# Agent attention and a squared-ReLU MLP on one core: key pieces three blocks apart, value pieces about nine, the cast of the exponentials on VectorE

## The chip, the core and the metric

The kernel runs on one core of one Trainium2 chip. The metric is the device time of one execution, in microseconds (us). The engines are named as the profile names them: PE is TensorE's matmuls, PEld its weight loads, DVE is VectorE, ACT is ScalarE, POOL is GpSimd, SP is SyncE, which here issues the DMAs.

## What is computed

The reference, cut to what matters (B = 4 batches, 12480 rows in each, 128 columns, 49 agents, 49920 tokens, a hidden width of 2048):

```python
def sm(a, b):
    s = scale * (a @ b.transpose(0, 2, 1))
    s = s - s.max(-1, keepdims=True)
    e = np.exp(s)
    return e / (e.sum(-1, keepdims=True) + 1e-09)
agent_v = sm(agents, k) @ v
x = (sm(q, agents) @ agent_v).reshape(B * S, D)
r = np.maximum(x @ w_in, 0.0)
return (r * r) @ w_out
```

A batch thus has two attention parts. The first goes over all its keys and values and ends in 49 rows, `agent_v`. The second takes its queries to the agents. The MLP then runs over all tokens, and it is nearly all of the matmul work.

## The kernel before

**Tiling.** A supertile is 960 tokens (120 partitions x 8 columns of tokens, `ST`); a batch has 13 of them, the whole run 52. Keys and values come in pieces of the same size, 13 a batch. The hidden width is cut in 16 slices of 128. One slice of one supertile is a block; there are 52 x 16 = 832 blocks, and they are the clock by which everything is ordered.

**A block.** `mm1` (L467) makes 128 x 960 hidden values in PSUM from the query probabilities `p_a`, `p_b` (49 rows) and the weights `w_a`, `w_b`, into which `agent_v @ w_in` has been folded. Products are kept near float32 by splitting each operand in a high and a low part of the type float32r and adding three products. So `mm1` is 6 matmuls of 480 columns and `mm2` 12. ACT does the ReLU (L471) and the square (L475), DVE casts the square to its high part `gh` (L479) and subtracts to get the low part `gl` (L483). `mm2` (L495) follows `LAG` = 6 blocks behind `mm1` and adds up 16 blocks in two PSUM banks, which `store_a` (ACT, L506) and `store_d` (DVE, L510) empty after each supertile.

**Beside the blocks.** For each supertile there is the query work: `q_half` (PE, L195, two halves of the scores), `q_shift` (DVE, L386 and L392), `q_exp` (ACT, L401), `q_total` (DVE, L405 to L409), `q_norm` (POOL, L412), `q_hi` (ACT, L420 and L421), `q_lo` (POOL, L425 and L426), `q_transpose` (PE, L436), `q_copy` (ACT, L442 and L443, into `p_a`) and `q_spread` (two DMAs that copy `p_a` into `p_b`). For batches 1 to 3 the key and value work of the batch is laid among the blocks of the batch before it. Batch 0 has none to hide behind; it is computed ahead of the first block.

**Keys.** Two pieces share one pass (`k_pair`, PE, L195, two halves of 32 small matmuls in the trace); `kp_copy` (ACT, L212) takes the scores to SBUF into `sk`, `kp_max` (DVE, L217) reduces them. After all 13 pieces `k_max` finds the maximum over the batch (L230 to L242).

**Values.** Only then can a value piece be done: `k_sub` (POOL, L245) subtracts the maximum, `k_exp` (ACT, L248) takes the exponential, `k_hi` (ACT, L252) casts it to its high part in the tile `pe`, `k_lo` (POOL, L255) makes the low part; `v_hi` (ACT, L262) and `v_lo` (DVE, L266), two halves each, split the values; `v_acc` (PE, L274, 16 matmuls) and `v_sum` (DVE, L281) add the product up. `a_final` and four `w_make` (L356 to L360) close the batch and make the next `w_a` and `w_b`.

**Order.** A planner writes the order. `at(t, f)` puts a step at block time `t`; `chain` (L534) looks for free places: at most one extra step on ACT, on DVE or on PE in a block (`taken`), and no two users of the attention PSUM banks at once (`banks`; there is one such pair of banks, the tile `ps_att`). All steps are then sorted by time and issued in this order, so each engine's queue has exactly that order. `plan_turns` (L588) places `q_transpose` at least `SLACK` = 5 blocks behind `q_lo`. `plan_batch` (L593) spreads a batch's key pieces and then its value pieces evenly, both by `d = (span - 50) / (2 * NS)`, which is 6.08 blocks for `span` = 208. With that, batch 1's keys end near block 74 of its 208, and its value pieces lie from block 79 to 169.

**Start.** Ahead of block 0, PE computes batch 0's attention, two `w_make`, and the scores of the first three key pieces of batch 1 (`AHEAD` = 3, by `k_scores`, L184, with ACT's L223 and DVE's L226). The weights come as float64 bits and are turned into float32 on DVE by `win_make` and `wo_make` (L91 to L97, seven instructions for each quarter).

Of the kernel before, what the change touches and what calls it, by code (L numbers as in the profile page):

```python
# [25 lines left out]
def agent_attention_relu2_kernel(ctx: ExitStack, tc: tile.TileContext, qT, kT, v, agT, w_in, w_out, outT):  # L26
# [6 lines left out]
    nc = tc.nc  # L33
    C, B, NCH, _ = kT.shape
# [138 lines left out]
    def piece(n):  # L173
        return sk[:, n * G:(n + 1) * G, :]
# [74 lines left out]

    def k_hi(n):  # L250
        pes[n] = wk.tile([CH, G, A2], F32R, name="pe", bufs=3)
        nc.scalar.copy(pes[n][:, :, :A], piece(n))  # L252

    def k_lo(n, eng=nc.gpsimd):
        eng.tensor_tensor(out=pes[n][:, :, A:], in0=piece(n), in1=pes[n][:, :, :A].bitcast(F32), op=ALU.subtract)  # L255
# [261 lines left out]

    LAG = 6
    SLACK = 5
    AHEAD = 3  # L520
    steps = []

    def at(t, f, *args):
        steps.append((t, len(steps), f, args))
# [9 lines left out]
    def chain(t, todo):  # L534

        first = prev = None
        while todo:
            n = 1  # L540
            while todo[0][0] == "PE" and n < len(todo) and (todo[n][1] in reads_bank and todo[n][0] != "PE" or todo[n][1:-1] == todo[n - 1][1:-1]):
                n += 1
            t += hop[prev][todo[0][0]] if prev else 0
            while True:
                g, p, ts = t, None, []
                for e, *_ in todo[:n]:
                    g += hop[p][e] if p else 0
                    while (e, g) in taken:
                        g += 1
                    ts.append(g)  # L550
                    p = e
                held = range(ts[0], ts[-1] + 2) if todo[0][0] == "PE" else ()
                if not any(y in banks for y in held):
                    break
                t += 1
            banks.update(held)
            for (e, f, *args), g in zip(todo, ts):
                taken.add((e, g))
                at(g + .5, f, *args)
            first = ts[0] if first is None else first  # L560
            prev, t, todo = p, ts[-1], todo[n:]
        return first, t
# [23 lines left out]
    ends = {}  # L586

    def plan_turns(s):  # L588
        _, end = chain(max(ends[s] + (1 if s < 3 else SLACK), (s - 1) * NF), [("PE", q_transpose, s), ("ACT", q_copy, s)])
        at(end + .9, q_spread, s)  # L590
        assert end + 3 < s * NF, (s, end)

    def plan_batch(b, base, span):  # L593

        d = (span - 50) / (2 * NS)
        n = AHEAD if b == 1 else 0
        while n < NS:
            m = min(2, NS - n)
            f = k_pair if m == 2 else k_one
            first, end = chain(base + int(n * d), [("PE", f, b, n, 0), ("PE", f, b, n, 1), ("ACT", kp_copy, n, m), ("DVE", kp_max, n, m)])  # L600
            for x in range(m):
                at(max(base, first - 8 + x), k_load, b, n + x)
            n += m
        _, t0 = chain(end + 1, [("DVE", k_max, 0, NS), ("PE", k_max, 2), ("DVE", k_max, 3), ("PE", k_max, 4), ("DVE", k_max, 5)])
        used = {}
        for n in range(NS):
            t = t0 + 1 + int(n * d)
            t2 = max(t + 3, used.get(n - 2, 0))
            first, _ = chain(t2, [("ACT", v_hi, n, 0), ("DVE", v_lo, n, 0)])
            _, t2 = chain(t2 + 1, [("ACT", v_hi, n, 1), ("DVE", v_lo, n, 1)])  # L610
            at(first - 6, v_load, b, n)
            chain(t - (3 if n else 0), [("POOL", k_sub, n)])
            _, t1 = chain(max(t + (2 if n else 3), used.get(n - 3, 0)), [("ACT", k_exp, n), ("ACT", k_hi, n), ("POOL", k_lo, n)])
            used[n], end = chain(max(t1 + SLACK, t2 + 2), [("PE", v_acc, n), ("DVE", v_sum, n)])
        _, end = chain(end + 1, [("DVE", v_join), ("DVE", a_final, 0), ("PE", a_final, 1), ("DVE", a_final, 2), ("DVE", a_final, 3)])
        for f in range(F // 512):
            _, end = chain(end + 2, [("PE", w_make, b, f, 0), ("ACT", w_make, b, f, 1), ("DVE", w_make, b, f, 2)])
        assert end + 2 < base + span, (b, end, base + span)
# [75 lines left out]
    for f in range(2):  # L694
        for x in range(3):
            at(t + 4 + .1 * x + .5 * f, w_make, 0, f, x)
    for n in range(AHEAD):
        at(t + 5 + .1 * n, k_scores, 1, n)
        at(t + 5.5 + .1 * n, k_copy, n)
        at(t + 5.5 + .1 * n, k_pmax, n)  # L700
    for x in range(7):
        at(t + 8 + .1 * x, wo_make, 1, x)
        at(1.52 + x, wo_make, 2, x)
    for x in range(2):
        at(.13 + .01 * x, wo_split, 0, x)
        at(1.56 + .01 * x, wo_split, 1, x)
        at(8.52 + x, wo_split, 2, x)
    at(t + 12, begin)
    at(1.95, warm_up, 3)
    at(3.95, warm_up, 2)  # L710
    plan_queries_early(1, 0, True)
    plan_turns(1)
    for f in range(2, F // 512):
        chain(4 * f - 7, [("PE", w_make, 0, f, 0), ("ACT", w_make, 0, f, 1), ("DVE", w_make, 0, f, 2)])
    _, end = chain(8, [("DVE", wo_make, 3, x) for x in range(7)] + [("ACT", wo_split, 3, 0)])
    at(end + .6, wo_split, 3, 1)
    assert end < 3 * PW // P + LAG
# [49 lines left out]
```

## Time and profile before

| | us |
|---|---|
| median of 3 runs | 2041.16 (2036.58 to 2042.4) |
| the profiled execution | 2041.42 |
| its span in the trace | 2039.6 |
| first ReLU of block 0 (L471) | at 78.15 |
| mean granted PE clock | 0.982 of full speed |

The profiled execution is the one that the rows below are from. 1.8 us of its time lie outside the span. A row of the timeline gives the start, the duration, the engine, the line and the operation, and in brackets how long the engine stood idle ahead of it and what ended that. A row of the stretches ("A:B length, ...") gives each engine's busy time in the stretch with the number of instructions in parentheses, then the granted PE clock, the share of DMA and the GB/s.

### The profile page before, as it was taken

Reading aid. Unit: us, or ns where it says so; the run is one execution under the profiler, and the core shown is the slowest. Engines: PE = TensorE matmul, PEld = TensorE weight load, DVE = VectorE, ACT = ScalarE, POOL = GpSimd, SP = SyncE. Lnnn points to the kernel's source line nnn. Section 1 sums busy time; section 2 is a strip of 40 time slices with the busy share of each in tenths; the row PEclk is TensorE's granted clock in tenths of the full one; section 3 lists DMA queues with packets and bytes.
Section 4 is the critical chain, followed back from the end, with each engine's and each line's share of the span. In section 5 each row is a group of like instructions: output and inputs, shape, how many; then the busy total and the mean of one; then the engine's idle time right before and its main releaser. Section 6 shows DMA issues by size and latency. Waiting matters only on the chain.

```text
span 2039.6 us, 47851 instructions
## 1 busy us (share of the span) xinstructions
PE 1995.0 (98%) x19791; PEld 1871.2 (92%) x19795; DVE 1787.5 (88%) x2267; ACT 1762.3 (86%) x2202; POOL 409.2 (20%) x261
## 2 busy tenths in 40 slices
PE   9899999999999999899999999989999999999998
PEld 8689998889899999898999999989898999999997
DVE  6798899889888889899988888989998898999887
ACT  2488899889888889898988888988998999999997
POOL 2110024443000002444201001245400101010100
PEclk8899999999999999999999999999999999999999
DMA  8321211120021211131011121122110010101000
GB/s 288 110 86 54 76 54 54 57 73 25 28 102 44 77 54 53 57 92 34 24 67 63 47 93 34 56 71 75 34 38 33 28 44 28 44 28 44 28 24 21
DMA packets 38503, 119.40 MB, mean 59 GB/s; under 512 B 4164, under 2 KB 11692, under 8 KB 38284
## 3 DMA queue, kind: packets, MB, share of 16 engines
q1 hardware_dynamic: 38284, 116.33, 17.7%
q8 instruction: 155, 2.54, 0.5%
q14 instruction: 64, 0.52, 0.1%
HBM read 80.97 MB, written 25.56 MB: 52 GB/s over the span
## 4 chain that ended last, share of the span: by engine, by line
PE 88%; ACT 4%; DVE 3%; issue 2%; POOL 2%; POOLq 0%; ACTq 0%; DVEq 0%
PE out L495 50%; PE h L467 24%; PE ps_att L195 7%; POOL pp L426 2%; PE ps_att L436 2%; PE ps_att L274 2%; ACT r L471 2%; ACT g L475 2%; PE h L184 1%; PE out L295 1%; DVE gl L483 1%; PE ps_att L356 1%; PE ps_one L184 1%; POOL e L412 1%; DVE gh L479 1%
## 5 line engine op out<-in xcount | busy, mean ns | idle before, releaser
L483 DVE TENSOR_TENSOR gl<-g,gh 128x960 fp32r<-128x960 f32 x832 | 987.2, 1187 | 0.0
L471 ACT ACTIVATE r<-h 128x960 f32<-128x960 f32 x832 | 810.3, 974 | 177.0 <-PE h L467 147.6
L495 PE MATMUL out<-gh,wo_hi 64*128 64x480 f32 x3328 | 862.6, 391 | 14.3 <-ACT ob L506 12.5
L495 PE MATMUL out<-gl,wo_hi 64*128 64x480 f32 x3328 | 843.4, 379 | 3.2 <-DVE gl L483 3.2
L495 PE MATMUL out<-gh,wo_lo 64*128 64x480 f32 x3328 | 844.4, 380 | 0.0
L475 ACT ACTIVATE g<-r 128x960 f32<-128x960 f32 x832 | 833.1, 1001 | 6.6 <-DVE gl L483 6.2
L479 DVE CAST gh<-g 128x960 fp32r<-128x960 f32 x832 | 596.3, 717 | 195.2 <-ACT g L475 125.6
L495 PEld LDWEIGHTS out<-gh,wo_hi 64*128 64x128 f32 x3328 | 480.6, 186 | 45.7 <-ACT ob L506 18.8
L495 PEld LDWEIGHTS out<-gl,wo_hi 64*128 64x128 f32 x3328 | 482.0, 186 | 21.1 <-DVE gl L483 4.7
L495 PEld LDWEIGHTS out<-gh,wo_lo 64*128 64x128 f32 x3328 | 485.6, 188 | 12.6
L467 PE MATMUL h<-p_a,w_a 49*128 49x480 f32 x1664 | 432.3, 390 | 0.1
L467 PE MATMUL h<-p_b,w_a 49*128 49x480 f32 x1664 | 423.9, 379 | 0.0
L467 PE MATMUL h<-p_a,w_b 49*128 49x480 f32 x1664 | 423.7, 379 | 0.0
L412 POOL TENSOR_TENSOR e<-e,sm 120x392 f32<-120x392 f32 x52 | 67.7, 1302 | 972.8 <-PE out L495 594.1
L467 PEld LDWEIGHTS h<-p_a,w_b 49*128 49x128 f32 x1664 | 242.5, 186 | 17.1
L467 PEld LDWEIGHTS h<-p_a,w_a 49*128 49x128 f32 x1664 | 240.7, 186 | 13.9 <-ACT r L471 4.5
L467 PEld LDWEIGHTS h<-p_b,w_a 49*128 49x128 f32 x1664 | 244.6, 189 | 7.2
L425 POOL TENSOR_TENSOR pp<-e,pp 120x196 fp32r<-120x196 f32 x52 | 89.2, 1715 | 242.2 <-PE out L495 144.4
L195 PEld LDWEIGHTS ps_att<-ag_sb,qt 64*120 64x120 f32 x1632 | 118.8, 186 | 3.0 <-DVE pm L226 0.8
L195 PE MATMUL ps_att<-ag_sb,qt 64*120 64x49 f32 x1632 | 111.7, 262 | 0.4 <-DVE pm L226 0.4
L255 POOL TENSOR_TENSOR pe<-sk,pe 120x392 fp32r<-120x392 f32 x39 | 78.9, 2027 | 151.1 <-PE out L495 112.9
L426 POOL TENSOR_TENSOR pp<-e,pp 120x196 fp32r<-120x196 f32 x52 | 104.0, 2001 | 0.0
(133 smaller groups left out, 1202.4 us busy)
## 6 DMA issues: line engine op xcount, KB each, us to landing
kt<-kT SPq DMA_DIRECT2D x52, 480.0 KB
vt<-v SPq DMA_DIRECT2D x52, 480.0 KB
qt<-qT SPq DMA_DIRECT2D x52, 480.0 KB
outT<-ob SPq DMA_DIRECT2D x51, 480.0 KB
p_b<-p_a SPq DMA_DIRECT2D x104, 91.9 KB
raw<-w_in SPq DMA_DIRECT2D x4, 512.0 KB
raw<-w_out SPq DMA_DIRECT2D x4, 512.0 KB
outT<-ob SPq DMA_DIRECT2D x2, 240.0 KB
```

Source lines behind the costliest of these rows:

```text
L184: nc.tensor.matmul(ps[:CH, c * A:(c + 1) * A], kt[:, c, :], ag_sb[:, b, :], start=True, stop=True)
L195: mm = nc.tensor.matmul(ps[:CH, u, r * A:(r + 1) * A], cols[u][r][rows], ag_sb[rows, b, :], start=x == 0 and r == 0, stop=x == 1 and r == ...
L255: eng.tensor_tensor(out=pes[n][:, :, A:], in0=piece(n), in1=pes[n][:, :, :A].bitcast(F32), op=ALU.subtract)
L412: eng.tensor_tensor(out=es[s], in0=es[s], in1=sms.pop(s).to_broadcast([CH, G, A]), op=ALU.mult)
L425: eng.tensor_tensor(out=pp[:, :H, 64:], in0=e[:, :H], in1=pp[:, :H, :A].bitcast(F32), op=ALU.subtract)
L426: eng.tensor_tensor(out=pp[:, H:, :A], in0=e[:, H:], in1=pp[:, H:, 64:].bitcast(F32), op=ALU.subtract)
L467: nc.tensor.matmul(hs[i][:, t, :TT], w, p, start=n == 0, stop=n == 2)
L471: nc.scalar.activation(rs_[i], hs.pop(i)[:, :, :TT], AF.Relu)
L475: nc.scalar.activation(gs[i], rs_.pop(i), AF.Square)
L479: nc.vector.tensor_copy(ghs[i], gs[i])
L483: nc.vector.tensor_tensor(out=gls[i], in0=gs.pop(i), in1=ghs[i].bitcast(F32), op=ALU.subtract)
L495: mm = nc.tensor.matmul(o[u][:, :TT], w[rows, j, :], g[rows, u, :], start=j == 0 and x == 0 and n == 0, stop=j == NF - 1 and x == 1 and n ...
```

## The change

Four edits, all but one of them in the planner.

```diff
     def k_hi(n):
         pes[n] = wk.tile([CH, G, A2], F32R, name="pe", bufs=3)
-        nc.scalar.copy(pes[n][:, :, :A], piece(n))
+        nc.vector.tensor_copy(pes[n][:, :, :A], piece(n))
...
+    KD, TAIL, EARLY = 3, 46, 4
...
-        _, end = chain(max(ends[s] + (1 if s < 3 else SLACK), (s - 1) * NF), [("PE", q_transpose, s), ("ACT", q_copy, s)])
+        _, end = chain(max(ends[s] + (1 if s < 3 else SLACK + 3), (s - 1) * NF), [("PE", q_transpose, s), ("ACT", q_copy, s)])
...
-        d = (span - 50) / (2 * NS)
-        n = AHEAD if b == 1 else 0
+        n = EARLY if b == 1 else 0
...
-            first, end = chain(base + int(n * d), [("PE", f, b, n, 0), ("PE", f, b, n, 1), ("ACT", kp_copy, n, m), ("DVE", kp_max, n, m)])
+            first, end = chain(base + int(n * KD), [("PE", f, b, n, 0), ("PE", f, b, n, 1), ("ACT", kp_copy, n, m), ("DVE", kp_max, n, m)])
...
+        d = (base + span - TAIL - t0) / (NS - 1)
...
-            _, t1 = chain(max(t + (2 if n else 3), used.get(n - 3, 0)), [("ACT", k_exp, n), ("ACT", k_hi, n), ("POOL", k_lo, n)])
+            _, t1 = chain(max(t + (2 if n else 3), used.get(n - 3, 0)), [("ACT", k_exp, n), ("DVE", k_hi, n), ("POOL", k_lo, n)])
...
-    for n in range(AHEAD):
-        at(t + 5 + .1 * n, k_scores, 1, n)
-        at(t + 5.5 + .1 * n, k_copy, n)
-        at(t + 5.5 + .1 * n, k_pmax, n)
     for x in range(7):
-        at(t + 8 + .1 * x, wo_make, 1, x)
-        at(1.52 + x, wo_make, 2, x)
+        at(t0 + 20.9 + .4 * x, wo_make, 1, x)
+        at(3.6 + .4 * x, wo_make, 2, x)
...
+    at(1.55, k_load, 1, AHEAD)
+    for n, t in ((0, 2.5), (2, 6.5)):
+        for x in range(2):
+            at(t + .6 * x, k_pair, 1, n, x)
+        at(t + 1, kp_copy, n, 2)
+        at(t + 1.05, kp_max, n, 2)
```

First, a batch's key pieces lie 3 blocks apart, a pair thus 6. The value pieces take what is left, `d` about 9.3 to 9.5 blocks apart: those of batch 1 lie from block 49 to 179, where they lay from 79 to 169. Second, `k_hi` goes from ACT to DVE. Third, `q_transpose` keeps three blocks more from `q_lo`; where the banks were taken, the planner went further still. Fourth, the scores of batch 1's first pieces leave the start: four pieces, as two pairs, come in blocks 2 to 7. `wo_make` of the second quarter of `w_out` moves ahead of block 0, that of the third is packed into blocks 3 to 6, the `w_make` of `w_in`'s last two quarters move to blocks 4 and 8, and three of the five filler matmuls in blocks 1 to 3 fall away.

The rows below are each engine's order in the built programs. ACT just ahead of block 0 and in it (a difference, - before, + after; L358 ends `w_make`, L223 copies scores of `k_scores`, L471 is the ReLU, L119 the high part of `w_out`):

```order
 L358 CAST w_a<-ps_one 113x512
 L358 CAST w_a<-h 113x512
-L223 COPY sk<-ps_one 120x392
-L223 COPY sk<-h 120x392
-L223 COPY sk<-ps_one 120x392
 L471 ACTIVATE r<-h 128x960
 L119 CAST wo_hi<-wo_f 128x512
```

The three score copies are gone, and with them three groups of scores on PE; block 0's ReLU follows the `w_make` at once.

ACT among batch 1's value pieces, before (from about block 91; L262 is `v_hi`, L248 the exponential, L252 `k_hi`, L471 and L475 the blocks' own work):

```order
L262 CAST vs_86<-vt 120x4x128
L471 ACTIVATE r<-h 128x960
L475 ACTIVATE g<-r 128x960
L248 ACTIVATE sk<-sk 120x392
L471 ACTIVATE r<-h 128x960
L475 ACTIVATE g<-r 128x960
L252 CAST pe<-sk 120x8x49
L471 ACTIVATE r<-h 128x960
L475 ACTIVATE g<-r 128x960
L248 ACTIVATE sk<-sk 120x392
L471 ACTIVATE r<-h 128x960
L475 ACTIVATE g<-r 128x960
```

and DVE there after (from about block 78; L252 is `k_hi`, L281 `v_sum`, L266 `v_lo`, L479 and L483 the blocks' own):

```order
L483 TENSOR_TENSOR gl<-g,gh 128x960
L479 CAST gh<-g 128x960
L252 CAST pe<-sk 120x8x49
L483 TENSOR_TENSOR gl<-g,gh 128x960
L479 CAST gh<-g 128x960
L281 TENSOR_TENSOR acc<-ps_att,acc 98x516
L483 TENSOR_TENSOR gl<-g,gh 128x960
L479 CAST gh<-g 128x960
L266 TENSOR_TENSOR vs_86<-vt,vs_86 120x4x128
```

`k_hi` is now one of DVE's four extra instructions for a value piece, and ACT's are three where they were four.

ACT around the copy of the transposes of supertile 7, before (L442 and L443 are `q_copy`, which stands right behind `q_transpose` in the plan; L506 is `store_a`):

```order
L442 CAST p_a<-ps_att 113x8x64
L443 CAST p_a<-ps_att 113x8x56
L471 ACTIVATE r<-h 128x960
L475 ACTIVATE g<-r 128x960
L248 ACTIVATE sk<-sk 120x392
L471 ACTIVATE r<-h 128x960
L475 ACTIVATE g<-r 128x960
L252 CAST pe<-sk 120x8x49
L471 ACTIVATE r<-h 128x960
L506 COPY ob<-out_3658 128x480
```

and after (L401 is `q_exp` of supertile 8):

```order
L471 ACTIVATE r<-h 128x960
L506 COPY ob<-out_3747 128x480
L475 ACTIVATE g<-r 128x960
L471 ACTIVATE r<-h 128x960
L475 ACTIVATE g<-r 128x960
L471 ACTIVATE r<-h 128x960
L475 ACTIVATE g<-r 128x960
L401 ACTIVATE e<-e 120x392
L471 ACTIVATE r<-h 128x960
L475 ACTIVATE g<-r 128x960
L442 CAST p_a<-ps_att 113x8x64
L443 CAST p_a<-ps_att 113x8x56
```

The transposes stood three blocks ahead of the store; now they stand three blocks behind it and behind the next supertile's query scores. In the plan that is block 98 before and 104 after, with `q_lo` at block 93 in both, and the first block that uses the result is 112.

More of the change, by code (lines that the diff above doesn't have):

```diff
@@ L706, in agent_attention_relu2_kernel @@
         at(1.56 + .01 * x, wo_split, 1, x)
-        at(8.52 + x, wo_split, 2, x)
+        at(9.52 + x, wo_split, 2, x)
     at(t + 12, begin)
-    at(1.95, warm_up, 3)
-    at(3.95, warm_up, 2)
+    at(1.95, warm_up, 2)
     plan_queries_early(1, 0, True)
     plan_turns(1)
+    at(1.55, k_load, 1, AHEAD)
[4 more added lines that the diff above has]
+        at(t + 1.05, kp_max, n, 2)
     for f in range(2, F // 512):
-        chain(4 * f - 7, [("PE", w_make, 0, f, 0), ("ACT", w_make, 0, f, 1), ("DVE", w_make, 0, f, 2)])
+        for x in range(3):
+            at(4 * f - 3.5 + .1 * x, w_make, 0, f, x)
+    banks.update(range(2, 10))
+    taken.update((e, t) for e in ("ACT", "DVE") for t in (3, 4, 7, 8))
     _, end = chain(8, [("DVE", wo_make, 3, x) for x in range(7)] + [("ACT", wo_split, 3, 0)])
```

## Prediction

> **What bounds the kernel now.** I read the page's shares and the chain that ended last, then the same engines stretch by stretch, then the timeline where a stretch is long.
>
> ```profile
> PE 1995.0 (98%) x19791; PEld 1871.2 (92%) x19795; DVE 1787.5 (88%) x2267; ACT 1762.3 (86%) x2202; POOL 409.2 (20%) x261
> PE 88%; ACT 4%; DVE 3%; issue 2%; POOL 2%; POOLq 0%; ACTq 0%; DVEq 0%
> ```
>
> PE is nearly always busy, but DVE and ACT are not far behind, so a stage can have another limit than the whole. The next rows are stretches of five supertiles among the value pieces of batches 1, 2 and 3, one supertile of batch 2's, one stretch with key pairs, and six supertiles of the last batch, which carry no key or value work. Columns: length, then busy time of PE, PEld, DVE, ACT, POOL.
>
> ```profile
> 275.20:475.40 200.20, 189.95 (x1875) 177.02 (x1872) 184.64 (x228) 180.04 (x242) 88.25 (x40) 0.97 0.20 60
> 776.60:976.70 200.10, 190.43 (x1875) 175.80 (x1873) 184.92 (x229) 180.03 (x242) 89.76 (x40) 0.97 0.20 60
> 1277.90:1478.40 200.50, 190.31 (x1875) 176.88 (x1873) 185.28 (x229) 180.11 (x242) 86.94 (x40) 0.97 0.20 60
> 852.50:896.70 44.20, 39.73 (x377) 37.90 (x375) 36.13 (x47) 36.53 (x51) 23.91 (x8) 0.92 0.17 50
> 624.70:662.20 37.50, 37.50 (x405) 35.91 (x403) 31.52 (x40) 32.75 (x40) 2.79 (x3) 1.00 0.17 59
> 1587.10:1791.30 204.20, 204.20 (x2022) 198.25 (x2020) 185.45 (x229) 191.54 (x229) 20.95 (x18) 1.00 0.11 36
> ```
>
> The ReLU's line alone, cut the same way, counts the blocks (its first row holds 80; the second holds 96 and the start of one more):
>
> ```profile
> 776.60:976.70 200.10, 78.01 (x80) 0.97 0.20 60
> 1587.10:1791.30 204.20, 93.45 (x97) 1.00 0.11 36
> ```
>
> Without key or value work a supertile takes 204.2 / 6 = 34.03 us, and PE has no gap: that is PE's pace. Key pairs keep it so (37.5 of 37.5 us busy). Among value pieces it is different. Five supertiles at PE's pace are 170.2 us; 12 `v_acc` fall in them, and one takes 0.96 us of the chain (row below), 11.5 us together. So PE needs 181.7 us and the stretch takes 200.1: **18.4 us a batch are not PE's work.** A second look at the same rows says why. ACT is busy for 180.0 us and DVE for 184.9, where the work without values takes 191.54 / 6 = 31.9 and 185.45 / 6 = 30.9 a supertile. Three engines need 180 to 185 us each; none can catch up when it has waited. The timeline shows the worst wait:
>
> ```profile
> 845.83 0.96 PE ps_att L274 x16
> ...
> 844.71 5.00 POOL L425 TENSOR_TENSOR pp<-e,pp 120x196 fp32r<-120x196 f32 x1 [2.70 <-ACT r L471]
> 849.68 11.70 POOL L426 TENSOR_TENSOR pp<-e,pp 120x196 fp32r<-120x196 f32 x1
> 861.34 0.94 POOL L245 TENSOR_TENSOR sk<-sk,mM 120x392 f32<-120x392 f32 x1
> ...
> 849.17 0.68 DVE L281 TENSOR_TENSOR acc<-ps_att,acc 98x516 f32<-98x516 f32 x1
> 859.76 1.15 DVE L483 TENSOR_TENSOR gl<-g,gh 128x960 fp32r<-128x960 f32 x1
> 866.96 0.66 DVE L479 CAST gh<-g 128x960 fp32r<-128x960 f32 x1 [6.05 <-ACT g L475]
> ...
> 861.43 0.97 PE L436 MATMUL ps_att<-ident_r,pp 64*113 64x64 f32 x8 [4.47 <-POOL pp L426]
> ```
>
> `q_lo`, two POOL operations, takes 16.7 us; it ends just after DVE has run dry (DVE's last instruction ends at 860.91, POOL's at 861.38). POOL gets on only when DVE leaves it room. PE stood 4.47 us for it, since the transposes are in PE's queue ahead of the blocks; that supertile took 44.2 us.
>
> **The change part by part.**
>
> *Value pieces apart.* They now take 130 blocks (49 to 179), 8.125 supertiles, not 80-odd. PE's own need there: 8.125 x 34.03 + 13 x 0.96 = 289.0 us. What a piece adds on the others comes from the batch 2 row: DVE (184.92 - 5 x 30.9) / 13 = 2.34 us (this holds what POOL takes from it), ACT (180.03 - 5 x 31.92) / 13 = 1.57 us.
>
> *The cast.* ACT is rid of 0.52 us a piece. DVE has no such cast in the trace; the nearest are these:
>
> ```profile
> L252 ACT CAST pe<-sk 120x392 fp32r<-120x392 f32 x39 | 20.3, 521 | 0.0
> L479 DVE CAST gh<-g 128x960 fp32r<-128x960 f32 x832 | 596.3, 717 | 195.2 <-ACT g L475 125.6 <-PE h L467 60.2 <-PE out L495 2.0
> L56 DVE CAST ident_r<-ident 128x128 fp32r<-128x128 f32 x1 | 0.2, 217 | 0.0
> ```
>
> 128 columns take 0.22 us and 960 take 0.72, so 392 take between these, 0.38 on the line through both (217 + 264 x 500 / 832 = 376 ns). Then DVE needs 8.125 x 30.9 + 13 x 2.72 = 286.4 us, 99% of PE's need, where it was 184.9 against 181.7, 102%. ACT: 8.125 x 31.92 + 13 x 1.05 = 273.0 us, 94%, where it was 99%. Queued behind the cast on DVE are the block's own `gh` and `gl`; it waits for the exponential, which ACT does in the same block, as `v_lo` already waits for `v_hi`.
>
> *The transposes.* They stand 11 blocks behind `q_lo` in the plan instead of 5, some 13 us more at 2.2 us a block, against the 4.47 us that PE stood. The 8.2 us that the supertile of 44.2 us took over its need (34.03 + 2 x 0.96 = 35.95) go with it. The cover at the other end: 7 blocks, 15 us, remain until `mm1` needs the result, and the copy into `p_b` must fit; in the start its DMA issue begins at 68.01 and `mm1` reads it at 77.51 without a wait, so it takes at most 9.5 us. If that cover went, PE would stand at the start of each supertile.
>
> *What is left of the 18.4 us.* The other 10.2 us are 2.04 a supertile, from ACT and DVE running at PE's own pace. At 94% and 99% I take half of it, 1.02 x 8.125 = 8.3 us. Bounds: nothing (with DVE at 185.45 of 204.2 us, 91%, PE shows no gap), and 16.6 us if the rate stays. So the value stretch gives back 18.4 - 8.3 = 10.1 us a batch, **30.3 us** in three; bounds 1.8 x 3 = 5.4 and 55.2.
>
> *Key pieces.* Each half costs PE 1.62 us wherever it stands (row below), so bunching them moves no work. At 6 blocks a pair, 2.67 pairs a supertile, PE needs 34.03 + 2.67 x 3.24 = 42.7 us, far above ACT and DVE. Batch 2's first pair stands half a block behind its loads in the plan, but a load waits only for its buffer and for what is ahead in SP's queue, the copy into `p_b` at block 200.9; in the trace loads follow that copy within a microsecond:
>
> ```profile
> 108.03 0.70 SPq L448 DMA_DIRECT2D p_b<-p_a  x1
> 109.34 1.22 SPq L178 DMA_DIRECT2D kt<-kT  x2
> ...
> DMA packets 38503, 119.40 MB, mean 59 GB/s; under 512 B 4164, under 2 KB 11692, under 8 KB 38284
> ...
> kt<-kT SPq DMA_DIRECT2D x52, 480.0 KB
> ```
>
> 480 KB at the 59 GB/s of the whole run are 8.3 us, and 7.6 blocks are 16. Cost: nothing.
>
> *The start.*
>
> ```profile
> 72.12 1.78 PE L184 MATMUL ps_one<-ag_sb,kt 128*120 128x49 f32 x16
> 77.19 0.48 PE L467 MATMUL h<-p_a,w_a 49*128 49x480 f32 x2
> 77.51 0.38 PE L467 MATMUL h<-p_b,w_a 49*128 49x480 f32 x2
> 67.72 0.28 DVE L322 TENSOR_TENSOR acc<-out,acc 49x129 f32<-49x129 f32 x1 [4.58 <-PE out L312]
> 72.08 0.69 DVE L360 TENSOR_TENSOR w_b<-ps_one,w_a 113x512 fp32r<-113x512 f32 x1 [1.82 <-ACT w_a L358]
> 78.36 0.42 DVE L91 TENSOR_SCALAR cv_p<-raw 128x512 uint32<-128x512 uint32 x1
> 83.25 0.65 DVE L479 CAST gh<-g 128x960 fp32r<-128x960 f32 x1
> 68.01 0.85 SPq L447 DMA_DIRECT2D p_b<-p_a  x1
> 78.10:120.70 42.60, 15.62 (x17) 0.84 0.12 41
> 144.44 1.62 PE ps_att L195 x32
> ```
>
> Block 0 began at 77.19, behind three score groups from 72.12 on. Without them it can begin when `w_b` is there, 72.08 + 0.69 = 72.77: 4.4 us earlier. `wo_make` of the second quarter held DVE from 78.36 to 83.25, ahead of block 0's cast; now it lies in the 4.58 us that DVE stood idle ahead of 67.72, so 4.9 us of DVE go from the first blocks. Against that four halves of 1.62 us, 6.5 us, come into them. Blocks 0 to 5 have no `mm2`, and the first 16 blocks took 42.6 us at a clock of 0.84, so PE has room; I take half of the 6.5 as hidden. That is 4.9 - 3.25 = 1.65. And the blocks later carry 9 pieces instead of 10, 1.6 us less. Together **7.6 us**; bounds: nothing hidden, 4.4, or all, 10.9.
>
> **Sum.** 2041.4 (profiled execution, 0.3 us above the median of 2041.16) - 30.3 - 7.6 = 2003.5, **2004 us**. By the bounds: 2041.4 - 55.2 - 10.9 = 1975, and 2041.4 - 5.4 - 4.4 = 2032.
>
> **A rule against it.** The Trainium skill, "SBUF — State Buffer", section "Who interferes with whom", says that GpSimd's only ports are VectorE's second pair, that a VectorE cast in a 2-port mode or an operation with two SBUF inputs holds it for the whole instruction, and that reductions, and operations with at most one SBUF input outside those modes, do not. The trace agrees: L425's 5.00 us ended at 849.71, in `v_sum`, which reads one operand from PSUM, and L426 then sat through casts and subtractions until DVE ran dry. By the rule `k_hi` on DVE shuts POOL out for longer; its outcome is the third rival.
>
> **The rivals.**
>
> 1. *PE alone sets the pace among the values.* For it: DVE at 91% costs nothing today. Against: 99% is not 91%. Then all 55.2 us go: 2041.4 - 55.2 - 7.6 = 1979. Chance 0.18.
> 2. *The waits only move.* POOL's `k_sub` and `k_lo` also wait for room, `k_exp` waits for `k_sub`, and the same 18.4 us a batch come back over more blocks: 2041.4 - 7.6 = 2034. For it: only the transposes get more cover, nothing else. Against: ACT has room now. Chance 0.10.
> 3. *DVE shuts POOL out in every supertile of values.* Then the loss goes with the supertiles, 18.4 / 5 x 8.125 = 29.9 us a batch, 11.5 more than now: 2041.4 + 34.5 - 7.6 = 2068, slower. It decides where DVE's need passes PE's: (289.0 - 286.4) / 13 = 0.2 us more a piece, a cast of 0.58 us instead of 0.38, inside its bounds. Against: between pieces more blocks are bare, and a bare block leaves DVE idle. Chance 0.08.
> 4. *The start brings nothing*, because the pairs hold up the first blocks: 2041.4 - 30.3 = 2011. Chance 0.07, inside the range.
>
> The forecast itself has 0.57.
>
> **How the numbers follow.** A measurement of this kernel can tell about 0.3% from no change, 6 us. Forecast, first and fourth rival are faster, 0.82; the second, 7 us under, lies at the edge: I put 0.05 to faster and 0.05 to no change. Slower has 0.08. The range leaves out half of the first rival at the bottom and the third at the top: 1982 to 2035.
>
> **What would show it.** Right: the value stretches near 297 us for 130 blocks, with PE busy over 97%; no POOL operation of over 10 us for which PE stands; block 0's ReLU near 74; `k_hi` on DVE near 0.38 us in the mean. Wrong: value supertiles over 37.5 us each, long waits for L245 or L255 in place of L426, waits at a supertile's first block, `k_hi` over 0.58 us.

## The result and the profile after

| | before | after |
|---|---|---|
| median of 4 runs, us | 2041.31 (2036.58 to 2042.4) | 2016.66 (2013.45 to 2019.05) |
| ratio, 95% interval | | 0.9883 [0.9859, 0.9906] |
| the profiled execution, us | 2041.42 | 2018.85 |
| its span, us | 2039.6 | 2017.1 |

The change makes the kernel 24.6 us faster, 22.6 by the two profiled executions. The forecast was 37. The page of after, shares and chain:

```profile
PE 1987.2 (99%) x19836; PEld 1869.0 (93%) x19840; DVE 1797.3 (89%) x2306; ACT 1750.2 (87%) x2162; POOL 333.0 (17%) x261
PE 89%; DVE 4%; ACT 3%; issue 2%; POOL 2%; POOLq 0%; ACTq 0%; DVEq 0%
```

The shares hardly tell the two kernels apart: DVE has a percent more of the span and of the chain; ACT has a percent more of the span and a percent less of the chain. POOL's 409.2 us of before, which hold its waiting for DVE inside an instruction, are now 333.0. The stretches tell more. Blocks and stretches are named here after the batch whose key and value work is laid among them: "batches 2 and 3" are blocks 208 to 623. First these 416 blocks of before (from block 208's ReLU to block 624's), then the same blocks of after, its value pieces of batches 2 and 3 (8 supertiles each, 12 `v_acc`), its worst supertile, and six supertiles without key and value work:

```profile
584.10:1587.10 1003.00, 983.13 (x10016) 922.35 (x10014) 885.00 (x1111) 885.07 (x1115) 229.93 (x130) 0.99 0.18 56
```

```profile
575.10:1565.10 990.00, 979.13 (x10016) 925.32 (x10014) 897.35 (x1137) 877.95 (x1088) 186.25 (x130) 0.99 0.18 56
699.40:998.80 299.40, 293.95 (x2895) 277.40 (x2893) 284.04 (x357) 272.24 (x343) 79.70 (x50) 0.98 0.17 52
1196.70:1491.20 294.50, 289.07 (x2893) 274.04 (x2891) 283.19 (x357) 271.99 (x343) 79.80 (x50) 0.99 0.18 53
880.50:922.60 42.10, 41.00 (x383) 37.25 (x381) 37.99 (x46) 34.54 (x44) 10.90 (x10) 0.92 0.13 41
1565.10:1769.10 204.00, 204.00 (x2021) 196.20 (x2019) 183.54 (x229) 191.14 (x229) 17.03 (x18) 1.00 0.11 36
```

PE's own pace is unchanged: 204.0 / 6 = 34.0 us a supertile. For 8 supertiles and 12 `v_acc` of 0.96 us it needs 283.5 us, so the value pieces of batch 2 lose 15.9 us and those of batch 3 lose 11.0, as do those of batch 1 (294.5 us too). Before, batch 2 lost 18.4; the forecast left 8.3.

The waits of before that the change was to remove, PE's wait for `store_a`, and those of after (engine, line, who was waited for: us in total, times, longest):

```profile
PE ps_att L436 <- POOL pp L426: 13.3, 3, 4.5
...
PE out L495 <- ACT ob L506: 12.5, 12, 1.7
...
ACT g L475 <- DVE gl L483: 6.2, 11, 0.9
```

```profile
ACT g L475 <- DVE gl L483: 21.1, 28, 1.4
...
PE out L495 <- ACT ob L506: 12.2, 14, 1.5
...
PE ps_att L195 <- DVE acc L281: 3.0, 3, 1.0
...
ACT pp L420 <- POOL e L412: 0.2, 1, 0.2
```

The transposes' wait is gone, as forecast. `q_hi`, which stands behind POOL's `q_norm`, waits for nothing worth naming. What has grown is another wait: ACT's square waits for a buffer that DVE's `gl` has yet to read, 21.1 us instead of 6.2. DVE is behind. PE itself now stands longest for ACT: `mm2` waits for `store_a` to empty a bank, 12.2 us in all, and 12.5 before. The prediction has no term for this wait, and the change leaves it as it was. The timeline shows where, in the worst supertile. DVE first, then POOL, then PE with its stretches:

```profile
880.17 0.98 DVE L479 CAST gh<-g 128x960 fp32r<-128x960 f32 x1
881.08 0.77 DVE L252 CAST pe<-sk 120x392 fp32r<-120x392 f32 x1
881.77 1.92 DVE L483 TENSOR_TENSOR gl<-g,gh 128x960 fp32r<-128x960 f32 x1
883.62 0.65 DVE L479 CAST gh<-g 128x960 fp32r<-128x960 f32 x1
884.19 1.45 DVE L266 TENSOR_TENSOR vs<-vt,vs 120x512 fp32r<-120x512 f32 x1
...
887.97 0.68 DVE L266 TENSOR_TENSOR vs<-vt,vs 120x512 fp32r<-120x512 f32 x1
888.57 1.14 DVE L483 TENSOR_TENSOR gl<-g,gh 128x960 fp32r<-128x960 f32 x1
```

```profile
881.59 1.09 POOL L255 TENSOR_TENSOR pe<-sk,pe 120x392 fp32r<-120x392 f32 x1
883.69 1.40 POOL L255 TENSOR_TENSOR pe<-sk,pe 120x392 fp32r<-120x392 f32 x1 [1.02 <-DVE gl L483]
```

```profile
892.58 1.04 PE L195 MATMUL ps_att<-ag_sb,qt 64*120 64x49 f32 x16 [0.95 <-DVE acc L281]
```

```profile
891.58:894.99 3.41, 2.31 (x26) 1.72 (x27) 3.41 (x6) 3.38 (x5) 0.00 (x0) 1.00 0.00 0
894.99:901.82 6.83, 6.83 (x44) 5.96 (x44) 5.21 (x7) 2.21 (x4) 0.00 (x0) 0.50 0.19 74
```

No DVE row has a bracket: it never pauses. `gl` takes 1.14 us undisturbed and 1.92 beside POOL's L255; `v_lo` takes 0.68 and 1.45. So each of these two POOL operations that got through cost DVE about 0.77 us. The cast, the splits and POOL operations of two pieces and of the queries stand together here, and at 892 PE's query scores wait for `v_sum`. Then the last two rows: in 3.41 us PE was busy for 2.31, and for the next 6.83 us its clock was granted at half. The pause itself cost 1.1 us, the half clock another 3.4.

That gives the ruler for all that follows. The matmuls of batches 2 and 3 are the same in every kernel, so two numbers can be read from their row: the length less PE's busy time is what PE stood, and its busy time above that of a run without half clock there is roughly what the clock cost. Roughly, because the ends of matmuls are modelled in the trace: half of the time that the traces show at half clock is 0.7 to 5.3 us less (13.7 us before and 8.5 after, where the table has 14.4 and 10.4). The sum of the two, the length above 968.74 us, does not depend on how it is split.

The start, first the rows of blocks 0 to 15, before and after, then the timeline of after:

```profile
78.10:120.70 42.60, 38.75 (x312) 30.12 (x311) 38.76 (x56) 33.65 (x43) 6.42 (x6) 0.84 0.12 41
```

```profile
73.90:121.30 47.40, 45.20 (x435) 37.58 (x436) 33.58 (x49) 34.85 (x44) 6.30 (x6) 0.86 0.21 68
```

```profile
73.89 0.97 ACT L471 ACTIVATE r<-h 128x960 f32<-128x960 f32 x1 [0.89 <-PE h L467]
79.13 3.40 PE L195 MATMUL ps_att<-ag_sb,kt 64*120 64x49 f32 x32 [1.23 <-issue]
```

Block 0 comes 4.3 us earlier (78.15 to 73.89), but the 16 blocks take 4.8 us longer. The first pair fell in a stretch of half clock: its halves took 3.40 and 3.35 us, twice the 1.62. Those of the second pair, at 94.86 and 98.52, took 1.78.

### The profile page after: what moved, and what is told of

Read it like the earlier page. It is cut to its first block, busy times and chain, and to the rows that moved or that the text cites. A ratio compares the mean times of both kernels' runs of the same rounds, so it can differ in the third digit from the quotient of the medians.

```text
span 2017.1 us, 48016 instructions
## 1 busy us (share of the span) xinstructions
PE 1987.2 (99%) x19836; PEld 1869.0 (93%) x19840; DVE 1797.3 (89%) x2306; ACT 1750.2 (87%) x2162; POOL 333.0 (17%) x261
## 4 chain that ended last, share of the span: by engine, by line
PE 89%; DVE 4%; ACT 3%; issue 2%; POOL 2%; POOLq 0%; ACTq 0%; DVEq 0%
PE out L495 51%; PE h L467 25%; PE ps_att L195 7%; PE ps_att L436 2%; DVE gl L483 2%; PE ps_att L274 2%; POOL sk L245 1%; DVE gh L479 1%; ACT r L471 1%; PE out L295 1%; PE h L184 1%; ACT g L475 1%; PE ps_att L356 1%; PE ps_one L184 0%; DVE vs L266 0%
## 5 line engine op out<-in xcount | busy, mean ns | idle before, releaser
L483 DVE TENSOR_TENSOR gl<-g,gh 128x960 fp32r<-128x960 f32 x832 | 982.7, 1181 | 0.0
L471 ACT ACTIVATE r<-h 128x960 f32<-128x960 f32 x832 | 812.4, 976 | 168.5 <-PE h L467 141.2
L495 PE MATMUL out<-gh,wo_hi 64*128 64x480 f32 x3328 | 887.1, 390 | 15.1 <-ACT ob L506 12.2
L495 PE MATMUL out<-gh,wo_lo 64*128 64x480 f32 x3328 | 867.4, 379 | 0.7 <-POOL wo_lo L121 0.7
L495 PE MATMUL out<-gl,wo_hi 64*128 64x480 f32 x3328 | 865.4, 378 | 0.0
L475 ACT ACTIVATE g<-r 128x960 f32<-128x960 f32 x832 | 835.1, 1004 | 21.4 <-DVE gl L483 21.1
L479 DVE CAST gh<-g 128x960 fp32r<-128x960 f32 x832 | 591.0, 710 | 168.9 <-ACT g L475 132.5
L495 PEld LDWEIGHTS out<-gh,wo_hi 64*128 64x128 f32 x3328 | 499.5, 185 | 48.4 <-ACT ob L506 19.7
L495 PEld LDWEIGHTS out<-gl,wo_hi 64*128 64x128 f32 x3328 | 500.8, 185 | 17.0 <-DVE gl L483 1.8
L495 PEld LDWEIGHTS out<-gh,wo_lo 64*128 64x128 f32 x3328 | 505.0, 187 | 12.3 <-POOL wo_lo L121 1.1
L467 PE MATMUL h<-p_b,w_a 49*128 49x480 f32 x1664 | 434.9, 377 | 0.0
L412 POOL TENSOR_TENSOR e<-e,sm 120x392 f32<-120x392 f32 x52 | 48.9, 941 | 1031.7 <-DVE gl L483 646.0
L425 POOL TENSOR_TENSOR pp<-e,pp 120x196 fp32r<-120x196 f32 x52 | 65.4, 1257 | 256.9 <-PE out L495 178.5
L255 POOL TENSOR_TENSOR pe<-sk,pe 120x392 fp32r<-120x392 f32 x39 | 71.9, 1844 | 131.5 <-PE ps_att L195 84.0
L245 POOL TENSOR_TENSOR sk<-sk,mM 120x392 f32<-120x392 f32 x39 | 74.3, 1906 | 100.6 <-PE out L495 76.6
```

Source lines behind the costliest of these rows:

```text
L245: eng.tensor_tensor(out=piece(n), in0=piece(n), in1=m.rearrange("p (o a) -> p o a", o=1).to_broadcast([CH, G, A]), op=ALU.subtract)
L412: eng.tensor_tensor(out=es[s], in0=es[s], in1=sms.pop(s).to_broadcast([CH, G, A]), op=ALU.mult)
L425: eng.tensor_tensor(out=pp[:, :H, 64:], in0=e[:, :H], in1=pp[:, :H, :A].bitcast(F32), op=ALU.subtract)
L467: nc.tensor.matmul(hs[i][:, t, :TT], w, p, start=n == 0, stop=n == 2)
L471: nc.scalar.activation(rs_[i], hs.pop(i)[:, :, :TT], AF.Relu)
L475: nc.scalar.activation(gs[i], rs_.pop(i), AF.Square)
```

## The experiments

The time of each kernel beside the kernel before on the same chip, and the ruler. Lengths are those of batches 2 and 3; "stood" is length less PE's busy time, "clock" PE's busy time less the 968.74 us of the run without the maximum's subtraction, whose PE clock was 1.00 there.

| kernel | us | before | ratio, 95% interval | length | stood | clock |
|---|---|---|---|---|---|---|
| before | | | | 1003.0 | 19.9 | 14.4 |
| after | 2016.66 | 2041.31 | 0.9883 [0.9859, 0.9906] | 990.0 | 10.9 | 10.4 |
| cast on ACT | 2007.95 | 2037.35 | 0.9851 [0.9829, 0.9873] | 979.5 | 7.8 | 3.0 |
| cast twice | 2057.51 | 2037.43 | 1.0087 [1.0060, 1.0113] | 1017.5 | 17.2 | 31.6 |
| distance alone | 2022.86 | 2037.43 | 0.9920 [0.9904, 0.9937] | 991.6 | 9.8 | 13.1 |
| spacing alone | 2033.62 | 2037.43 | 0.9982 [0.9968, 0.9996] | 1004.9 | 25.6 | 10.6 |
| old distance | 2050.07 | 2037.35 | 1.0058 [1.0039, 1.0076] | 1009.4 | 23.4 | 17.2 |
| spacing, late copy | 2014.44 | 2037.24 | 0.9880 [0.9861, 0.9898] | 986.4 | 10.6 | 7.1 |
| cast on ACT, late copy | 2009.14 | 2037.24 | 0.9852 [0.9835, 0.9868] | 987.7 | 10.6 | 8.4 |
| no subtraction | 1989.64 | 2037.43 | 0.9771 [0.9750, 0.9792] | 970.9 | 2.2 | 0 |
| old start | 2018.45 | 2037.35 | 0.9902 [0.9877, 0.9927] | 993.3 | 11.1 | 13.5 |
| more filler | 2016.55 | 2037.35 | 0.9891 [0.9872, 0.9911] | 990.0 | 10.8 | 10.4 |
| cast on ACT, more filler | 2008.60 | 2037.24 | 0.9851 [0.9834, 0.9868] | 979.4 | 7.5 | 3.2 |
| spacing and distance | 2003.92 | 2037.24 | 0.9823 [0.9804, 0.9841] | 979.6 | 7.5 | 3.4 |

**The cast back on ACT.** The changed kernel, with the cast's edit undone:

```diff
-        nc.vector.tensor_copy(pes[n][:, :, :A], piece(n))
+        nc.scalar.copy(pes[n][:, :, :A], piece(n))
...
-            ... [("ACT", k_exp, n), ("DVE", k_hi, n), ("POOL", k_lo, n)])
+            ... [("ACT", k_exp, n), ("ACT", k_hi, n), ("POOL", k_lo, n)])
```

> The changed kernel with one part undone: the cast k_hi is on ACT again, all else as changed. The changed kernel took 2016.7 us, 24.7 less than before. Theory A (what is left of the loss among the value pieces comes from dense runs of extra DVE steps, blocks 117 to 141 and 146 to 158 of a batch, where DVE's own work plus what POOL takes from it exceeds PE's): DVE loses three casts of 0.36 us in a dense run and ACT, at 94% of PE's need, takes them; 2009 to 2017 us, the two supertiles of 38 to 42 us shrink. Rival B (the move of the cast is what paid, since ACT was the engine without room): ACT goes back towards 99% and the loss of before returns in part, over 2022 us.

It took 2007.95 us, a little under Theory A's range. Its row of batches 2 and 3, and its wait of the square for DVE:

```profile
576.50:1556.00 979.50, 971.71 (x10014) 923.12 (x10012) 888.53 (x1111) 885.94 (x1114) 179.21 (x130) 1.00 0.18 56
```

```profile
ACT g L475 <- DVE gl L483: 4.8, 12, 0.8
```

Without the cast DVE is busy for 8.8 us less in 26 pieces, 0.34 each, and the two batches are 10.5 us shorter. The square waits 4.8 us for DVE, not 21.1. The rival, that ACT has no room for the cast, falls: ACT is busy for 885.9 us, as before the change, and nothing is the worse for it. The whole time gains 6.5 us by the ratios, and the two intervals still overlap; in the profiled start of this kernel the clock was half for longer (below). This pair alone does not settle the cast. With the cast on ACT the planner also lays other steps in other blocks: counted in the two traces, 87 of DVE's 603 instructions beside the blocks' own, the `v_sum` of 30 pieces and 24 of the 78 `v_lo` among them.

**The cast issued twice.** The other way round, on the changed kernel:

```diff
-        nc.vector.tensor_copy(pes[n][:, :, :A], piece(n))
+        for _ in range(2):
+            nc.vector.tensor_copy(pes[n][:, :, :A], piece(n))
```

> The changed kernel with the cast k_hi issued twice on DVE, 39 more instructions of 0.36 us. Moving the cast to ACT took 6 us off. Theory A (DVE is the engine without room among the values): the second cast costs as much again or more, 5 to 12 us, a ratio to before of 0.991 to 0.994. Rival B (DVE has room and the 6 us came from something else, such as where the planner put the steps): under 2 us, a ratio of 0.989 or less.

It took 2057.51 us, by the ratios 42 us more than the change. The lines count one more from L253 on. Its group of casts, its row of batches 2 and 3, and two stretches in a row out of batch 2:

```profile
L253 DVE CAST pe<-sk 120x392 fp32r<-120x392 f32 x78 | 36.0, 462 | 1.6
```

```profile
586.20:1603.70 1017.50, 1000.29 (x10016) 932.39 (x10014) 908.92 (x1163) 879.99 (x1089) 160.91 (x130) 0.97 0.17 54
...
835.29:838.70 3.41, 1.95 (x22) 1.25 (x19) 3.41 (x5) 3.38 (x6) 1.32 (x1) 1.00 0.00 0
838.70:845.53 6.83, 6.72 (x42) 5.93 (x44) 5.29 (x8) 1.73 (x2) 0.95 (x1) 0.50 0.47 146
```

The 26 added casts keep DVE busy for 11.6 us more, and the batches take 27.5 us more: 1.06 us for each cast. Every other step of DVE and ACT stands in the same block as in the change, so this run shows what the cast by itself does: DVE has no room. The expected 5 to 12 us were missed by far, and the ruler says why: PE stood only 6.3 us longer, but its clock cost 21.2 us more (18.8 by the time at half clock). The last two rows are one such case of eight in these batches.

**The transposes' distance alone.** The kernel before, with one edit of the change:

```diff
-        ... (ends[s] + (1 if s < 3 else SLACK), (s - 1) * NF) ...
+        ... (ends[s] + (1 if s < 3 else SLACK + 3), (s - 1) * NF) ...
```

> The kernel before with the transposes alone moved: SLACK + 3. Theory A (PE's stand for q_lo goes, 8 us a batch by the supertile of 44 us, but DVE and ACT stay as dense as before): 2012 to 2025 us. Rival B (the stall is a symptom of DVE and POOL in dense blocks and comes back elsewhere): 2033 to 2045 us.

```profile
577.50:1569.10 991.60, 981.85 (x10015) 924.52 (x10013) 881.57 (x1111) 883.51 (x1114) 184.07 (x130) 0.99 0.18 56
```

It took 2022.86 us, 16 us off by its ratio, and PE stood half as long, 9.8 us instead of 19.9. No wait of PE for L426 is left. The one number moves more than the transposes: after it the planner also lays 165 of DVE's 603 extra instructions in other blocks, so the 16 us are those of the distance and of these places together.

**The spacing alone.** The kernel before, with the change's two spacings (`d` for the keys replaced by 3, `d` for the values as in the change) and all else as it was.

> The kernel before with the spacing alone: key pieces 3 blocks apart, value pieces over what is left; cast on ACT, transposes 5 blocks behind q_lo, old start. Theory A (what costs time is where extra steps of DVE and ACT and POOL's operations fall together; the wider spacing thins them): 2012 to 2025 us. Rival B (the spacing brings nothing by itself; the distance of the transposes did it all, as the changed kernel without it, 12 us slower than before, suggests): 2035 to 2052 us.

It took 2033.62 us, 4 us off, near Rival B. Its row of batches 2 and 3, its waits, and a place in batch 3 on POOL, ACT and DVE:

```profile
573.90:1578.80 1004.90, 979.29 (x10016) 916.40 (x10013) 884.64 (x1111) 886.10 (x1114) 209.56 (x130) 0.99 0.18 56
```

```profile
ACT pp L420 <- POOL e L412: 30.5, 11, 3.8
PEld h L467 <- ACT r L471: 21.5, 17, 2.7
```

```profile
1260.11 6.30 POOL L412 TENSOR_TENSOR e<-e,sm 120x392 f32<-120x392 f32 x1 [1.07 <-PE out L495]
```

```profile
1266.44 0.36 ACT L420 CAST pp<-e 120x196 fp32r<-120x196 f32 x1 [3.76 <-POOL e L412]
```

```profile
1268.85 0.66 DVE L479 CAST gh<-g 128x960 fp32r<-128x960 f32 x1 [3.14 <-ACT g L475]
```

POOL's `q_norm` takes 6.30 us here, where its shortest in this run takes 0.84; it ends 0.7 us after DVE has run dry. `q_hi`, which ACT was to do next, waits 3.76 us for it with the blocks' ReLU and square behind it, then DVE waits 3.14 for the square, and PE for the ReLU. In the kernel before, `q_hi` waits 6.5 us in all for `q_norm`, here 30.5. That fits `q_norm` meeting dense runs of DVE more often, with the pieces in their new places; no run moved `q_norm` alone.

**The old distance in the changed kernel.** `SLACK + 3` set back to `SLACK`.

> The changed kernel with the transposes at 5 blocks behind q_lo again. Theory A (the wait of PE for q_lo came from a dense run of DVE steps; with the wider spacing POOL gets through, and the extra blocks matter little): within 4 us of 2016.7. Rival B (the distance of the transposes is what took PE's waits for L426 away): the stall of over 5 us a batch comes back, 2030 us or more.

```profile
587.40:1596.80 1009.40, 985.96 (x10016) 918.15 (x10014) 898.47 (x1137) 878.58 (x1089) 170.46 (x130) 0.99 0.18 56
```

```profile
ACT pp L420 <- POOL e L412: 22.2, 7, 4.0
PEld h L467 <- ACT r L471: 13.4, 14, 2.6
```

It took 2050.07 us, by the ratios 36 more than the change. But PE did not wait for L426 at all, nor does it with the spacing alone; the waits are again those of `q_hi` for `q_norm`. The reason for the distance's gain in the prediction, that the transposes no longer stand for `q_lo`, holds for the kernel before, not here. With the longer distance the planner finds other places for what it lays later, and in the changed kernel `q_hi` waits 0.2 us in all. Whether the distance or those places do it was not separated.

**The copy behind `q_norm` later.** If that is so, then the spacing alone should gain with `q_hi` three blocks later:

```diff
-  "POOL": {"PE": 1, "ACT": 0, "DVE": 0, "POOL": 1}}
+  "POOL": {"PE": 1, "ACT": 3, "DVE": 0, "POOL": 1}}
```

> The kernel before with the change's spacing of key and value pieces alone (which took 2034 us), and q_hi, the ScalarE copy that waits for q_norm on GpSimd, placed three blocks later. Theory A (with the spacing alone the time is lost because q_norm, stretched by VectorE from about 1.1 us to over 6, holds up q_hi at the head of ScalarE's queue, and behind it the next ReLU and with it TensorE): the wait of q_hi for L412, 30.5 us over 11 waits, goes nearly to nothing, TensorE's wait for the ReLU, 36 us together, falls under 10, and the time comes to 2015 to 2025 us, near what the longer distance of the transposes brings. Rival (GpSimd's operations are late as a whole, so the wait only moves to q_lo and the transposes, which stand behind it at the same distance as before): 2030 to 2038 us, with waits of TensorE for L426 in place of those for the ReLU.

```profile
572.90:1559.30 986.40, 975.80 (x10014) 928.43 (x10012) 894.41 (x1110) 884.70 (x1114) 158.43 (x131) 0.99 0.18 56
```

```profile
PEld h L467 <- ACT r L471: 1.8, 4, 0.8
ACT pp L420 <- POOL e L412: 0.2, 1, 0.2
```

It took 2014.44 us, 19 less than the spacing alone; both waits are nearly gone, and PE stood 10.6 us instead of 25.6. No wait for L426 took their place. This fits the account that the spacing lost its gain to an instruction at the head of an in-order queue, waiting for a starved POOL. It does not prove it alone: what stands behind `q_hi` in the plan moves with it, and in the traces 357 of ACT's 538 extra instructions and 153 of DVE's 603 are in other blocks. The same edit on the changed kernel with the cast on ACT, where that wait is gone already:

> The changed kernel with the cast back on ScalarE (2008 us) and q_hi three blocks later. Theory A (what is left of the loss among the value pieces is VectorE's own time and what GpSimd takes from it, not a copy that blocks ScalarE's queue, since that wait is already nearly gone there): 2005 to 2011 us, no difference that a measurement tells. Rival (short waits of q_hi still cost ScalarE time in each value supertile): 1998 to 2004 us.

It took 2009.14 us beside 2007.95, no difference, as this theory has it. It is not that the edit does nothing, though: in the profiled runs its batches 2 and 3 are 8.2 us longer, and its first 16 blocks end at 116.9 us instead of 126.0, by the clock of the start.

**No subtraction of the maximum.** The changed kernel without `k_sub` for batches 1 to 3, so that the exponentials are taken of the bare scores:

```diff
-            chain(t - (3 if n else 0), [("POOL", k_sub, n)])
```

> The changed kernel without k_sub for batches 1 to 3, so the exponentials are taken without the maximum subtracted (this part is left out); POOL has 39 operations of 0.9 to 1.9 us fewer, DVE's own work is the same. Theory A (POOL's operations cost DVE about 0.75 us each where DVE has no gap, and this is what makes the dense blocks late): the supertiles of 38 to 42 us fall under 37.5, 8 to 16 us less than the changed kernel, a ratio to before of 0.980 to 0.984. Rival B (DVE's own steps alone make them late): under 3 us, a ratio of 0.987 or more.

```profile
563.40:1534.30 970.90, 968.74 (x10016) 925.32 (x10014) 881.27 (x1137) 876.50 (x1089) 138.77 (x104) 1.00 0.18 57
```

It took 1989.64 us, 23 us less than the change by the ratios. That is more than Theory A's 16. All other steps of DVE and ACT stand in the same blocks. 26 POOL operations fewer take 16.1 us off DVE's busy time, 0.62 us each, in the measure of the 0.77 above; PE stands for 2.2 us in all, its clock is full, and a batch takes 485 us. A rival would be that `k_exp` no longer waits for `k_sub`, but in the change that wait is 2.4 us in all. PE's wait for `store_a` falls from 12.2 us to 3.0, though ACT does the same work in the same order:

```profile
PE out L495 <- ACT ob L506: 3.0, 7, 0.7
```

ACT's square waits 5.0 us for DVE here, 21.1 in the change. So `store_a` was late behind a late DVE, and what the change leaves of the loss is DVE's time with what POOL takes of it.

**The start.** The changed kernel with the start of before (with `EARLY` = 3 and all the lines of the start as they were):

> The changed kernel with the old start: three key pieces of batch 1 ahead of block 0 by k_scores, wo_make and w_make where they were; spacing, cast and transposes as changed. Theory A (the start brought nothing: the 4.3 us that block 0 comes earlier are given back in blocks 2 to 7, where the pairs run at half clock, 3.4 us a half pair instead of 1.6): 2015 to 2019 us, no difference to 2016.7. Rival B (the start brought its 7.6 us and the values less than it seems): 2022 to 2026 us.

It took 2018.45 us, ratio 0.9902 [0.9877, 0.9927] beside the change's 0.9883 [0.9859, 0.9906]: the intervals overlap, the new start is not told from the old. (With the cast on ACT the old start has 0.9823 [0.9804, 0.9841], below, and the new 0.9851 [0.9829, 0.9873]; these overlap too, the other way round.) Then the changed kernel with more filler matmuls ahead of the first pairs:

```diff
-    at(1.95, warm_up, 2)
+    at(1.95, warm_up, 8)
```

> The changed kernel with 8 filler matmuls in place of 2 at block 1.95, where PE waited 1.2 us for DVE and the clock then fell to half for 13.7 us. Theory A (the pairs in blocks 2 to 7 cost twice because of the half clock): the clock stays at full there, a half pair costs 1.6 us, and 5 us go, 2010 to 2013 us. Rival B (the first blocks are held by the chain PE, ACT, DVE and not by the clock): no gain, or 1 us more for the fillers.

It took 2016.55 us, as without. Then the same on the kernel with the cast on ACT:

> The changed kernel with the cast back on ScalarE (which took 2008 us) and eight instead of two filler matmul groups in the start. Theory A (the start's gain is eaten by a stretch of half clock that falls into the first blocks, and filler moves it before block 0, where the profiled start of the filler run had none): blocks 0 to 15 fall from 47 or more to about 43 us, block 0 comes 2 to 3 us later, and the time is 2003 to 2007 us. Rival (the half-clock stretch only moves or changes from run to run, and filler pays for itself at best): 2007 to 2011 us, no difference that a measurement tells.

2008.60 us, nothing again. Blocks 0 to 15 in three runs, more filler, the cast on ACT, and (old start) spacing and distance:

```profile
76.60:119.20 42.60, 40.28 (x441) 33.62 (x442) 33.80 (x49) 34.69 (x44) 7.05 (x6) 1.00 0.24 75
```

```profile
70.90:126.00 55.10, 52.91 (x436) 42.92 (x436) 33.70 (x49) 34.94 (x44) 7.88 (x6) 0.72 0.18 58
```

```profile
80.30:119.30 39.00, 34.50 (x311) 26.58 (x311) 38.55 (x56) 34.06 (x42) 6.52 (x6) 0.96 0.21 69
```

Block 16 begins at 119.2, 126.0 and 119.3 us, at 121.3 in the changed kernel and at 120.7 before. Over all the profiles it begins between 116.3 and 126.0 with the new start, and between 113.5 and 120.7 with the old. The new start begins up to 9 us earlier and is not, as a rule, farther on at block 16.

**Spacing and distance, nothing else.** The kernel before with both edits, the cast on ACT and the old start:

> The kernel before with the change's spacing and the longer distance of the transposes, the cast on ScalarE and the old start. It closes the table: the distance alone took 16 us off, the spacing alone 4, the cast on VectorE costs about 6, and all but the cast took 30 off. Theory A (the spacing is worth more once the transposes stand farther off, because then a late GpSimd operation stops nobody, and the new start brings 0 to 4 us): 2008 to 2012 us. Rival (distance and spacing merely add, and the new start brings the missing 8 to 10 us as the prediction said): 2017 to 2020 us.

```profile
570.00:1549.60 979.60, 972.11 (x10016) 927.06 (x10014) 888.79 (x1111) 885.06 (x1114) 182.80 (x130) 1.00 0.18 56
```

2003.92 us, under both theories' ranges and the fastest of the kernels that compute all of it: its interval lies wholly under that of the change. The kernel that differs from it in the cast, and in the places that the planner changes with it, is the one with the old start: 993.3 us for the two batches, 13.7 more, and 16 us more by the ratios of the whole. The spacing, 4 us alone, takes 20 more off what the distance alone had.

## Why the prediction was right in its sign and short in its size

The profiled span fell by 22.5 us. Cut at block 0 (78.1 and 73.9), block 16, and batches 2 and 3 as above, it fell by 4.2 up to block 0, by -4.8 in blocks 0 to 15, by 9.6 in the rest of batch 1, 13.0 in batches 2 and 3, 0.5 in the last. The rest of batch 1, before and after:

```profile
120.70:584.10 463.40, 452.77 (x4579) 425.84 (x4581) 414.63 (x521) 410.68 (x522) 119.57 (x66) 0.99 0.18 56
```

```profile
121.30:575.10 453.80, 447.12 (x4546) 420.65 (x4544) 418.43 (x536) 406.54 (x509) 94.18 (x66) 1.00 0.19 59
```

The prediction had 30.3 for the value stretches, which gave 9.6 + 13.0 = 22.6, and 7.6 for the start, which gave -0.6 (1.6 of the 7.6, one key piece less, lies in the rest of batch 1; counted there it raises the start to 1.0 and lowers the values to 21.0).

*The sum: closer than its parts.* The runs lead from before to after by four single steps. By the ratios the distance alone takes 16 us off, the spacing on top of it 20; the cast on VectorE then adds 16, and the new start takes 4 off, which the intervals do not tell from nothing. The prediction had 8.2 a batch for the transposes, 24.6 us, then 10.1 less 8.2 a batch for spacing and cast together, 5.7 us, and 7.6 for the start. That spacing and cast come out near this, at 4 us, is luck: the spacing gained 20, and the cast, which was counted as part of the gain, lost 16.

*The transposes: right, but for more than one reason.* The wait for L426 went, and `mm1` does not wait at a supertile's first block in its place. In the changed kernel the distance, with the places that go with it, is worth 36 us, where 8.2 a batch had been counted for it, and the wait that is absent with it there is that of `q_hi`, which stops ACT behind `q_norm`. The prediction saw POOL starved, and did not ask which other instruction waits in order for a POOL operation.

*The cast: the step that failed.* The prediction took ACT's relief, 99% to 94%, as part of the gain and DVE's 99% of PE's need as bearable. Its duration was about right (0.36 us in the median, 0.47 in the mean, against 0.38), and the third rival, by which POOL would be shut out, stayed away:

```profile
L252 DVE CAST pe<-sk 120x392 fp32r<-120x392 f32 x39 | 18.4, 471 | 0.2
L245 POOL TENSOR_TENSOR sk<-sk,mM 120x392 f32<-120x392 f32 x39 | 74.3, 1906 | 100.6 <-PE out L495 76.6 <-DVE mM L242 24.0
```

L245 takes 1906 ns here and 2060 with the cast on ACT. But the kernels with the cast take 5 to 7 us a batch longer than those without, and the cast issued twice, with all else in place, took 27.5 us more in two batches. ACT with the cast did not set the pace once the pieces lay apart; DVE did, because a need of 99% is a mean over 130 blocks, and in clumps it is above PE's pace: from 880 to 892 us DVE was busy for 11.99 of 12.00 us. With the cast on ACT the loss left in batches 2 and 3, stood and clock together, is (7.8 + 3.0) / 2 = 5.4 us a batch; with the change it is (10.9 + 10.4) / 2 = 10.6, where before had 17.2. The first is under, the second over the 8.3 that "half of it" allowed.

*The price of a wait: left out.* The 18.4 us a batch were read as PE standing. By the ruler, of the 34.3 us that the two batches of before lost, some 14 were clock. The prediction had a row with 0.92 in it, the supertile of 44.2 us, and took nothing from it. In the table each us of standing comes with up to 1.8 us of clock, most often 0.4 to 1.3: an estimate that adds up standing alone leaves that out.

*The start: mis-sized.* The 4.4 us by which block 0 comes earlier were right (4.3). The rest was not: half of the pairs' 6.5 us was to be hidden, and 4.9 us to be gained on DVE, 8.1 together. In blocks 0 to 15 PE was busy for 45.20 us, 6.45 more than before (38.75), and it stood for 2.20 us instead of 3.85. So hiding and DVE's relief gave 1.65 us, and 6.45 less 1.65 are the 4.8 that the blocks took longer. PE had stood for 3.85 us in all before; 8.1 could not come out of its pauses. Half clock does not explain the difference, since it took about as much before: 0.16 of 42.60 us, 6.8, against 0.14 of 47.40, 6.6. That the start brings nothing, the fourth rival, is what the runs show within what they can tell.

*The keys.* Nothing in any run speaks against their price of nothing; it was not tried alone.

## What to carry to other kernels

Read what a wait costs from a pair of stretches, the pause and the granted clock behind it, and not from the list of waits alone. When engines run within a few per cent of each other, it is the spacing and the distance of steps that gain, and moving an instruction to the engine which already sets the pace in dense places can lose, however small it is: here a cast of 0.36 us, 13 times a batch, was a loss of 5 to 7 us a batch. Behind a GpSimd operation that VectorE can starve, keep everything that waits for it in an in-order queue a few blocks away.

## What the runs showed of the hardware that was not expected

Half clock follows short pauses of PE. In the rows above PE was busy for 2.31 and 1.95 of 3.41 us, with no single wait over 1 us, and the next 6.83 us were granted at half, which cost 3.4 us. The traces have 44 such stretches of 3.41 or 6.83 us in batches 2 and 3. Ahead of two, both in the kernel before, PE stood for the whole 3.41 us; ahead of the other 42 it stood for 0.86 to 2.24 us of them. Cut into steps of 3.41 us that begin and end where these stretches do, the traces have 30 steps in which PE stood for over 1.3 us, and half clock followed all of them; it followed 14 of the 48 with 0.85 to 1.3 us, and none with less. This is found in the rows of thirteen kernels; no run set a pause by itself. The Trainium skill, "TensorE: Matmul & The Clock Gate", has in the section "HAM oscillation — how this bites in real kernels" the rule that no idle gap of PE should pass about 3.4 us. The traces here do not agree: PE stood for 1.1 and 1.5 us of the 3.41 ahead, and half clock followed. The same page of the Trainium skill gives the gate a window of 3413 ns in the section "Part 1: The HAM clock gate (the "warmup" mystery)"; the lengths of 3.41 and 6.83 us agree with it.

In the start the half clock differs from profile to profile of kernels that do the same work there: 0.72 of full clock in blocks 0 to 15 with the cast on ACT, 0.86 with the change, and 0.89 without the subtraction and with the cast twice. The 16 blocks took 55.1, 47.4, 45.7 and 45.8 us. A gain of some us in a start is not to be read from one profile.
